# A new order of the steps on each engine, with margins behind the transposing DMAs

## The chip, the cores and the metric

The kernel runs on one core of a Trainium2 chip. The metric is the device time of one execution in microseconds (us). A core has TensorE (PE; its weight loads are listed as PEld), VectorE (DVE), ScalarE (ACT), GpSimd (POOL) and SyncE (SP), each of which works through its own list of instructions in order, and 16 DMA engines. Nearly all DMAs of this kernel are issued by SP. About 0.2% of the time is what a measurement of this kernel can tell from no change.

## The reference

The input x is 8 x 4160 x 192, with 8 heads of 24 channels. For each of the 33280 positions and each head, seven taps (softmax of `weight_gen` over the taps) weigh the position and the six before it. The result goes through a gated layer with 1024 hidden channels.

```python
w = softmax(weight_gen)                        # over 7 taps
a = einsum('bshk,bskhg->bshg', w, x_unf)       # x_unf: the position and six before it
h = a @ w_in                                   # 192 -> 1024
e = exp(h - max(h)); sm = e / (sum(e) + 1e-9)
solu = h * sm
ln = (solu - mean(solu)) / sqrt(var(solu) + 1e-6) * g_ln
out = ln @ w_out                               # 1024 -> 192
```

## The kernel before

Each of the 128 partitions holds a run of 260 consecutive positions. Position t of all runs together is tile t: 128 rows, one of each partition. x and `weight_gen` come in chunks of 16 tiles (a first one of 4), so the work repeats every 16 tiles.

For each group of four tiles (pairs at the start) POOL multiplies x by the taps (step `attA`, line 180) and adds part of the seven products (`attB`, L195); for some groups DVE adds the rest (`fin`, L461). PE turns two tiles at a time (`xT`, L477; where more than one product is left it sums them as it turns them), ACT and DVE split the result into two f16 parts (`xhi` L487, `xld` L491), and two small DMAs make a copy with halves swapped (`sw`, L497).

Then each tile t runs through this chain:

- `mm1` (PE, L511 and L516): the first product, 12 matmuls into a PSUM tile h, of which there are three.
- `max` (DVE, L528), `exp` (ACT, L534), `solu` (DVE, L542), `sq` (ACT, L548).
- `hi` (ACT, L555) and `lo` (DVE, L559) write h as two f16 halves into a tile `hl`, of which there are three. So `hi` of tile t may start only when the transpose of tile t-3 has landed, and `mm1` of tile t+3 only when `sq` and `lo` of tile t are done.
- `tr` (SP, L567): a DMA that transposes `hl` (128 x 2048 f16) into `hlT`, of which there are six.
- `mm2` (PE, L607): the second product, 24 matmuls from `hlT` into the one PSUM tile po; `out` (ACT, L618) scales it and frees po for the next `mm2`; `od` (SP, L622) stores four tiles.

Small steps `f0` to `f5` (ACT and DVE on `stats`) work out scales for four tiles, `v0` to `v5` and `t0` to `t6` prepare a chunk (L109 to L169; `t6` on POOL, L124, waits for `t5` on DVE, L122), and SP loads the next chunk in one piece for the taps (`lw`, L93) and four for x (`lx0` to `lx3`, L87).

The order of the steps on each engine is not written out by hand. `plan` lists all steps with engine, an assumed duration and what each comes after. `issue_order` then plays them through: each engine takes, of the steps whose predecessors are done by its own account, the one with the lowest key. The key is t plus a number from the table `URGENCY` (by the name of the step, or by name and tile for tiles 0 to 11). Of a DMA its account is a queue: for `tr` 625 ns in the queue, 650 ns, 1792 ns of transfer behind earlier transfers, and 950 ns, some 4.0 us when nothing else is under way. `MARGIN` adds to the time at which a step counts as ready, by the first two letters of the step before it and of its own, for tiles above 11:

```python
late = MARGIN.get((step[0][:2], to[0][:2]), 0) if to[1] > 11 else 0
...
key = [round(t + URGENCY.get(f"{name}_{t}", URGENCY.get(name, 0)), 6) for name, t, *_ in steps]
...
add("hi", t, ACT, 907, ("solu", t), ("tr", t - 3))
add("lo", t, DVE, 1140, ("hi", t))
add("tr", t, SP, 1792, ("lo", t), ("mm2", t - 6))
```

The order that comes out is issued; the instructions of a step, their tiles and their semaphores' sense do not depend on it.

Of the kernel before, what the change touches and what calls it, by code (L numbers as in the profile page):

```python
# [26 lines left out]
def tile_kernel(ctx: ExitStack, tc: tile.TileContext, x, weight_gen, w_in, w_out, g_ln, out):  # L27
# [646 lines left out]


URGENCY = dict(
    a00=105.6, a01=-44.5, a02=-89.4, a03=47.5, a04=67.9, a10=-22.3, a11=-196.9, a12=96.5, a13=145.9,
    a14=177.2, attA=54.9, attA_0=-160.1, attA_2=-41.9, attA_4=31, attA_6=-19.2, attA_8=-123.4,
    attB=-205.9, attB_0=-169, attB_2=78.4, attB_4=68.1, attB_6=172.9, attB_8=18.9, b0=179.7,
    b1=203.8, b2=103.9, b3=75.4, b4=-60.5, c00=230, c01=36.5, c02=-94.8, c10=16.599, c11=-151.7,  # L680
    c12=-32.1, c20=111.7, c21=-219.8, c22=-108.5, c30=95.7, c31=-78.4, c32=-191, dup=57.3,
    dup_0=0.9, dup_2=-49.2, dup_4=18.3, dup_6=109.3, dup_8=-102.8, exp=-77.6, exp_0=-74.8, exp_1=45,
    exp_10=41.6, exp_11=-71, exp_2=128.8, exp_3=106.7, exp_4=86.8, exp_5=-4.3, exp_6=-75.7,
    exp_7=-4.1, exp_8=-11.5, exp_9=-3.7, f0=160.2, f0_1=3.2, f0_11=-40.2, f0_3=20.6, f0_5=24.8103,
    f0_7=114.5, f1=-36.7, f1_1=-165.1, f1_11=-170.3, f1_3=-0.6, f1_5=-249.6, f1_7=167.7, f2=49.2,
    f2_1=-243.1, f2_11=-14, f2_3=-69.7, f2_5=-55.4, f2_7=179.9, f3=-243.7, f3_1=141.5, f3_11=-172.4,
    f3_3=-104.6, f3_5=-83.7, f3_7=-40.4, f4=-134.3, f4_1=132.7, f4_11=233.9, f4_3=241.4,
    f4_5=-100.1, f4_7=-19.9, f5=-125.6, f5_1=-121.6, f5_11=2.6, f5_3=5, f5_5=-56.4, f5_7=-110,
    fin=191.2, hi=31, hi_0=-142.6, hi_1=103.6, hi_10=-67.5, hi_11=90.6, hi_2=221.7, hi_3=74.4,
    hi_4=28.6816, hi_5=-54.3, hi_6=-41.8, hi_7=89.3, hi_8=154, hi_9=-98.6, lo=127.7, lo_0=21.7,  # L690
    lo_1=-24.2, lo_10=112.1, lo_11=-179.4, lo_2=56.8, lo_3=-11.4, lo_4=89.3, lo_5=-8.3, lo_6=-21.9,
    lo_7=-247.5, lo_8=-163.7, lo_9=-44.9, lw=-190.9, lx0=18.1, lx1=-49.4, lx2=186.6, lx3=-8.2,
    max=153.7, max_0=79.6, max_1=121.7, max_10=198.3, max_11=-116.8, max_2=99.9, max_3=-205.4,
    max_4=174.9, max_5=186.6, max_6=59.1, max_7=-243.1, max_8=-234.1, max_9=-26, mm1=-16.5,
    mm1_0=98.6, mm1_1=32.3, mm1_10=-45.3, mm1_11=-44.6, mm1_2=-182.6, mm1_3=41, mm1_4=177.5,
    mm1_5=188, mm1_6=-114.6, mm1_7=55.6, mm1_8=-65.6, mm1_9=77.9, mm2=-9, mm2_0=190.3, mm2_1=43.9,
    mm2_10=168.7, mm2_11=-13, mm2_2=-182.9, mm2_3=-48.7, mm2_4=-38.6, mm2_5=106, mm2_6=-59.1,
    mm2_7=134.4, mm2_8=184.4, mm2_9=28.1, n0=-101, n1=180.7, n2=115.5, n3=-82.1, n4=-13.1, n5=-87.1,
    n6=41.8, n7=-57.7, nq=-111.6, od=-168.9, od_11=48.8, od_3=202.8, od_7=-0.7, out=-68.9,
    out_0=179.4, out_1=69.3, out_10=214.4, out_11=-86.2, out_2=-19.4632, out_3=122.7, out_4=79.1,  # L700
    out_5=42.2, out_6=30.8, out_7=-123.8, out_8=56.1, out_9=-24.6, p30=-124.8, p31=-234.5, p4=69.7,
    p5=-12, p6=71.4, p70=134.1, p71=57.4, p80=-77.1, p81=-139.6, p9=14.5, q00=187.9, q01=203.8,
    q02=-72.2, q10=3.2, q11=70.5, q12=-1.9, q20=-26.1, q21=-76.9, q22=-33.3, q30=0.1, q31=13,
    q32=-12.7, solu=-183.4, solu_0=31.5, solu_1=-72.3, solu_10=71.4, solu_11=-178.3, solu_2=-78.7,
    solu_3=132.8, solu_4=-28.5, solu_5=58.6, solu_6=156.9, solu_7=65.1, solu_8=-95.3, solu_9=137.7,
    sq=98.5, sq_0=84.5, sq_1=61.5, sq_10=107.4, sq_11=-148.9, sq_2=72.8, sq_3=214.1, sq_4=15.9,
    sq_5=20.8, sq_6=76.5, sq_7=-91.5, sq_8=243.3, sq_9=135.1, sw=184.3, sw_0=150, sw_10=2.4,
    sw_2=180.1, sw_4=195.8, sw_6=116.8, sw_8=-155.7, t0=112.6, t0_0=1.1, t0_4=-124.5, t1=176.6,
    t1_0=-41, t1_4=49.9, t2=55.9, t2_0=-140.2, t2_4=145.3, t3=-133.3, t3_0=-99.3, t3_4=75.3,
    t4=87.9, t4_0=147.5, t4_4=41.3, t5=-14.2, t5_0=75.8, t5_4=58.5, t6=10.8, t6_0=-64.7, t6_4=-82.4,  # L710
    tr=-16.4, tr_0=-96.7, tr_1=-162.1, tr_10=190.2, tr_11=-176.7, tr_2=-146.3, tr_3=-51.4,
    tr_4=-237.3, tr_5=-44.8, tr_6=5, tr_7=65.2, tr_8=226.7, tr_9=-111.3, v00=-103.7, v00_0=107.8,
    v00_4=-243.9, v01=34.5, v01_0=140.6, v01_4=-205.3, v02=110.9, v02_4=155.8, v03=118,
    v03_4=-117.1, v1=-95.7, v1_0=-136.3, v1_4=-116.9, v2=54.7, v2_0=-48.6, v2_4=138.2, v3=154.5,
    v3_0=-43.2, v3_4=46.8, v4=167.3, v4_0=0.4, v4_4=101, v5=175.4, v5_0=68.5, v5_4=-56.5, w0=-17.7,
    w1=136.2, x0=13.6, x1=-60.7, xT=-189.8, xT_0=-82.9, xT_10=12.1, xT_2=-42.7, xT_4=57.1,
    xT_6=-124.6, xT_8=-5.9, xhi=-9.1, xhi_0=-36.3, xhi_10=30.9, xhi_2=54.2, xhi_4=1.6, xhi_6=-85.3,
    xhi_8=-197.1, xld=247.4, xld_0=-3.8, xld_10=59.3, xld_2=138.7, xld_4=-134.5, xld_6=-25.9,
    xld_8=-1.3,
)  # L720


# [207 lines left out]
def held(t):  # L930
# [8 lines left out]
}  # L939


# [102 lines left out]
```

## Time and profile before

| | us |
|---|---|
| median of 3 runs | 1261.78 (1260.18 to 1262.72) |
| the profiled execution | 1261.43 |
| its span, first to last instruction | 1259.7 |

Busy share of the span: PE 95%, DVE 91%, POOL 91%, ACT 89%. A share is an average: at the start PE waits for the weights and the first groups, and in the last stretch POOL has nothing left to do. In between the work repeats with each chunk of 16 tiles, so a chunk is the natural unit to compare: how long it takes, how much of that PE is busy, and which wait makes one chunk longer than another. The instruction of DVE that adds up the last products of a group (L461) appears once at the same place of each chunk on the chain that ended last, and its start marks the chunks in the rows below.

### The profile page before, as it was taken

Reading aid. Unit: us, or ns where it says so; the run is one execution under the profiler, and the core shown is the slowest. Engines: PE = TensorE matmul, PEld = TensorE weight load, DVE = VectorE, ACT = ScalarE, POOL = GpSimd, SP = SyncE. Lnnn points to the kernel's source line nnn. Section 1 sums busy time; section 2 is a strip of 40 time slices with the busy share of each in tenths; the row PEclk is TensorE's granted clock in tenths of the full one; section 3 lists DMA queues with packets and bytes.
Section 4 is the critical chain, followed back from the end, with each engine's and each line's share of the span. In section 5 each row is a group of like instructions: output and inputs, shape, how many; then the busy total and the mean of one; then the engine's idle time right before and its main releaser. Section 6 shows DMA issues by size and latency. Waiting matters only on the chain.

```text
span 1259.7 us, 27355 instructions
## 1 busy us (share of the span) xinstructions
PE 1196.3 (95%) x10296; PEld 820.8 (65%) x10296; DVE 1151.4 (91%) x1777; ACT 1124.0 (89%) x2286; POOL 1140.3 (91%) x235
## 2 busy tenths in 40 slices
PE   2899999999999999999999999999999999999997
PEld 2466666666666666666666666666666666766667
DVE  7788989989999998999999999989999998999983
ACT  6689999988999999899999989989998999988885
POOL 5999999999999999999999999998999999999300
PEclk9899999999999999999999999999999999999999
DMA  7579797987979788797989879797998969868765
GB/s 241 120 172 220 143 215 147 194 158 171 205 142 222 154 194 164 171 211 140 224 158 191 175 165 205 144 213 151 188 177 176 207 138 210 151 140 145 149 148 122
DMA packets 585491, 219.18 MB, mean 174 GB/s; under 512 B 548623, under 2 KB 566031, under 8 KB 585102
## 3 DMA queue, kind: packets, MB, share of 16 engines
q1 hardware_dynamic: 585056, 216.32, 82.9%
q8 instruction: 81, 1.33, 0.4%
q10 hardware_dynamic: 302, 1.11, 0.3%
q14 instruction: 52, 0.43, 0.1%
HBM read 45.60 MB, written 25.56 MB: 56 GB/s over the span
## 4 chain that ended last, share of the span: by engine, by line
ACT 31%; PE 25%; DVE 21%; issue 13%; DMA 8%; POOL 1%; ACTq 0%; SPq 0%; DVEq 0%; POOLq 0%
PE po L607 9%; ACT hl L555 9%; ACT e L534 9%; PE h L516 7%; ACT e L548 7%; DMA hlT<-hl 7%; DVE h L542 6%; DVE hl L559 6%; PE h L511 4%; DVE h L528 4%; DVE a L461 4%; PE pa L477 3%; ACT ot L618 2%; ACT stats L594 1%; ACT junk L145 1%
## 5 line engine op out<-in xcount | busy, mean ns | idle before, releaser
L180 POOL TENSOR_TENSOR pr<-xt,wt 128x5376 f32<-128x5376 f32 (+1 forms) x67 | 631.2, 9420 | 0.2
L607 PE MATMUL po<-w_hl,hlT 128*128 128x192 f16 x6168 | 554.0, 247 | 21.4 <-ACT ot L618 20.1
L607 PEld LDWEIGHTS <-hlT 128*128 128x128 f16 x6240 | 525.2, 98 | 71.5 <-issue 33.2
L195 POOL TENSOR_TENSOR pr<-pr 128x2304 f32<-128x2304 f32 (+1 forms) x122 | 449.6, 3686 | 7.3
L559 DVE SCALAR_TENSOR_TENSOR hl<-h,hl 128x1024 f16<-128x1024 f32 x260 | 316.8, 1220 | 43.5 <-ACT hl L555 24.2
L555 ACT ACTIVATE hl<-h 128x1024 f16<-128x1024 f32 x260 | 267.4, 1029 | 90.0 <-DVE h L542 44.1
L528 DVE TENSOR_SCALAR_CACHE_REDUCE h<-h,row 128x1024 f32<-128x1024 f32 x260 | 334.0, 1285 | 11.3 <-PE h L516 10.5
L542 DVE SCALAR_TENSOR_TENSOR h<-h,row,e 128x1024 f32<-128x1024 f32 x260 | 333.8, 1285 | 10.7 <-ACT e L534 7.7
L534 ACT ACTIVATE e<-h,stats 128x1024 f32<-128x1024 f32 x260 | 292.1, 1123 | 5.6 <-DVE h L528 5.4
L548 ACT ACTIVATE e<-h,stats 128x1024 f32<-128x1024 f32 x260 | 291.9, 1123 | 1.3 <-DVE h L542 1.1
L516 PEld LDWEIGHTS <-xh 128*128 128x128 f16 x1560 | 131.5, 98 | 234.2 <-issue 111.8
L516 PE MATMUL h<-w_odd,xh 128*128 128x512 f16 x780 | 190.9, 381 | 0.0
L516 PE MATMUL h<-wa_hi,xh 128*128 128x512 f16 x520 | 178.2, 384 | 0.0
L618 ACT ACTIVATE ot<-po,stats 128x192 f32<-128x192 f32 x257 | 110.5, 430 | 10.2 <-PE po L607 10.1
L511 PE MATMUL h<-w_odd,turned 64*128 64x512 f16 x390 | 106.4, 380 | 4.8 <-DVE hl L559 2.7
L511 PE MATMUL h<-w_odd,xh 64*128 64x512 f16 x390 | 106.7, 380 | 0.0
L511 PE MATMUL h<-wb_hi,xh 64*128 64x512 f16 x260 | 99.5, 383 | 6.4 <-DVE hl L559 3.1
L477 PE MATMUL pa<-ident,pr 128*128 128x128 f32 x738 | 94.7, 276 | 6.6 <-POOL pr L180 4.3
L511 PE MATMUL h<-wb_hi,turned 64*128 64x512 f16 x260 | 99.6, 383 | 0.8 <-DMA turned<-xh 0.8
L516 PE MATMUL h<-wa_lo,xh 128*128 128x512 f16 x260 | 99.1, 381 | 0.0
L477 PEld LDWEIGHTS pa<-ident,pr 128*128 128x128 f32 x738 | 84.5, 143 | 14.4 <-POOL pr L180 5.2
L511 PEld LDWEIGHTS <-turned 64*128 64x128 f16 x780 | 54.2, 94 | 43.6 <-issue 23.8
(90 smaller groups left out, 1001.7 us busy)
## 6 DMA issues: line engine op xcount, KB each, us to landing
out_dram<-ot SPq DMA_DIRECT2D x64, 384.0 KB, 3.2
xt<-in_x_dram SPq DMA_DIRECT2D x30, 576.0 KB, 4.9
xt<-in_x_dram SPq DMA_DIRECT2D x30, 480.0 KB, 4.6
turned<-xh SPq DMA_DIRECT2D x260, 32.0 KB, 2.5
wt<-in_weight_gen_dram SPq DMA_DIRECT2D x16, 448.0 KB, 4.5
hlT<-hl SPq DMA_TRANSPOSE x260, 4.6
xt<-in_x_dram SPq DMA_DIRECT2D x1, 1536.0 KB, 10.9
pr<-in_moe_w_out_dram SPq DMA_DIRECT2D x1, 1024.0 KB, 8.2
```

What stands on the lines that cost most here:

```text
L180: nc.gpsimd.tensor_tensor(out=window(pr, 0, [(ROW, K), (HG, n * H), (1, HG)]), in0=window(xt, t * D, [(D, K), (HG, n * H), (1, HG)]), in1= ...
L195: nc.gpsimd.tensor_tensor(out=b, in0=b, in1=a, op=ALU.add)
L477: nc.tensor.matmul(pa[:, k], source[:, first : first + P], ident, is_transpose=True, start=at == 0, stop=at == 3 * len(sources) - 1,)
L511: nc.tensor.matmul(h[:, fs], last[(f + odd) % 2][rows, low], rhs[rows], start=n == 0, stop=False)
L516: nc.tensor.matmul(h[:, fs], xh[:, 2 * odd, low], rhs[:, fs], start=False, stop=n == 2)
L528: nc.vector.tensor_scalar(h, h, row(t, BACK), 3.0e38, op0=ALU.mult, op1=ALU.min, accum_out=stat(t, NMAX))
L534: nc.scalar.activation(e, h_of[t], AF.Exp, bias=stat(t, NMAX), scale=-1.0, accum_out=stat(t, Z))
L542: nc.vector.scalar_tensor_tensor(out=h, in0=h, scalar=row(t, SCALE), in1=e, op0=ALU.mult, op1=ALU.mult, accum_out=stat(t, M))
L548: nc.scalar.activation(e_of.pop(t), h_of[t], AF.Square, bias=stat(t, M), scale=-float(FF), accum_out=stat(t, Q),)
L555: nc.scalar.activation(hl[:, 0, :], h_of[t], AF.Copy, scale=2.0**14)
L559: nc.vector.scalar_tensor_tensor(out=hl[:, 1, :], in0=h_of[t], scalar=2.0**14, in1=hl[:, 0, :], op0=ALU.mult, op1=ALU.subtract,)
L607: nc.tensor.matmul(po[:, :D], hlT[:, half * NJ + j, :], w2_hl[:, j, w, :], start=n == 0, stop=n == len(terms) - 1,)
```

## The change

All numbers of `URGENCY` that belong to a step that exists are drawn anew, save some that stay as they were, and `MARGIN` gets two more entries: behind `tr`, 2500 ns ahead of `hi` and 2000 ns ahead of `mm2` (the letters "mm"). No step is added, removed or altered; only the order in which the engines' instructions, SP's DMAs among them, are issued. The names that the diff leaves at the same number are partly names that no step has. Core of the diff, first the lines of the table that hold the keys of the chain, of SP's steps and of PE's:

```diff
@@ URGENCY = dict(
...
-    fin=191.2, hi=31, hi_0=-142.6, hi_1=103.6, hi_10=-67.5, hi_11=90.6, hi_2=221.7, hi_3=74.4,
-    hi_4=28.6816, hi_5=-54.3, hi_6=-41.8, hi_7=89.3, hi_8=154, hi_9=-98.6, lo=127.7, lo_0=21.7,
...
-    lo_7=-247.5, lo_8=-163.7, lo_9=-44.9, lw=-190.9, lx0=18.1, lx1=-49.4, lx2=186.6, lx3=-8.2,
-    max=153.7, max_0=79.6, max_1=121.7, max_10=198.3, max_11=-116.8, max_2=99.9, max_3=-205.4,
...
+    f5_5=-56.4, f5_7=130, fin=85.7, hi=-31.1, hi_0=2.9, hi_1=90, hi_10=111.9, hi_11=202.5,
...
+    lo=-87, lo_0=-144.9, lo_1=33.8, lo_10=-216.8, lo_11=-104.9, lo_2=-4.8, lo_3=81.7, lo_4=89.7,
+    lo_5=26.6, lo_6=75.2, lo_7=-43.1, lo_8=5, lo_9=-108.5, lw=94.3, lx0=12.4, lx1=-31.5, lx2=-203.1,
+    lx3=99.1, max=54.6, max_0=-76, max_1=-140.8, max_10=170.3, max_11=205.2, max_2=-63.7,
...
@@ MARGIN = {
     ("lx", "v0"): 6000, ("lw", "t0"): 6000, ("lx", "at"): 6000, ("t0", "t1"): 6000,
     ("t1", "t2"): 3000, ("t2", "t3"): 3000, ("t3", "t4"): 3000, ("v2", "t4"): 3000,
     ("t5", "t6"): 6000, ("sw", "mm"): 6000, ("xl", "sw"): 1500, ("mm", "tr"): 1000,
+    ("tr", "hi"): 2500, ("tr", "mm"): 2000,
 }
```

Other keys that the text below speaks of, before and after: `exp` -77.6 and 97.9, `out` -68.9 and -0.5, `sq` 98.5 and 118.2, `solu` -183.4 and -63, `xld` 247.4 and 114, `tr` -16.4 and -106.8, `od` -168.9 and 73.8, `sw` 184.3 and 6.4, `mm1` -16.5 and -18.1, `mm2` -9 and -10.1.

## Rows read from the trace of the kernel before

**Rows 1.** The page, part 1: busy time of each engine and its share.
```profile
PE 1196.3 (95%) x10296; PEld 820.8 (65%) x10296; DVE 1151.4 (91%) x1777; ACT 1124.0 (89%) x2286; POOL 1140.3 (91%) x235
```

**Rows 2.** Windows by chunk: stretch, its length, busy us per engine, granted clock, DMA.
```profile
220.60:297.04 76.44, 73.19 (x628) 50.17 (x626) 70.02 (x108) 67.94 (x139) 75.97 (x16) 0.98 0.87 173
...
444.02:518.44 74.42, 71.90 (x627) 49.08 (x625) 69.84 (x108) 67.80 (x139) 71.21 (x15) 1.00 0.85 178
...
590.92:662.84 71.92, 71.68 (x627) 48.98 (x625) 69.67 (x109) 67.96 (x139) 71.26 (x15) 1.00 0.89 183
...
810.89:886.61 75.72, 73.45 (x627) 50.16 (x625) 70.03 (x108) 68.02 (x139) 71.21 (x15) 0.98 0.88 174
...
sum 812.70, PE 793.76 PEld 542.00 DVE 768.50 ACT 746.61 POOL 791.15; mean PE 72.16 PEld 49.27 DVE 69.86 ACT 67.87 POOL 71.92
```

**Rows 3.** Waits, whole span: who waited for whom, us in total, times, longest us.
```profile
ACT hl L555 <- DVE h L542: 44.1, 41, 1.7
...
DVE hl L559 <- ACT hl L555: 24.2, 28, 3.4
ACT hl L555 <- DMA hlT<-hl: 21.9, 12, 3.5
...
PE po L607 <- ACT ot L618: 20.1, 19, 3.0
...
PE h L511 <- DVE hl L559: 5.8, 18, 1.5
```

**Rows 4.** Waits in the quiet chunk, 590.92 to 662.84 us.
```profile
ACT hl L555 <- DVE h L542: 2.4, 2, 1.6
...
DVE hl L559 <- ACT hl L555: 0.3, 1, 0.3
```

**Rows 5.** Timeline of ACT, DVE, PE at 477 to 481 us: start, us, what, [idle before].
```profile
477.70 1.02 ACT L555 ACTIVATE hl<-h 128x1024 f16<-128x1024 f32 x1 [2.71 <-DMA hlT<-hl]
...
479.99 0.42 ACT L618 ACTIVATE ot<-po,stats 128x192 f32<-128x192 f32 x1
...
478.76 1.22 DVE L559 SCALAR_TENSOR_TENSOR hl<-h,hl 128x1024 f16<-128x1024 f32 x1 [2.47 <-ACT hl L555]
...
480.46 2.14 PE L607 MATMUL po<-w_hl,hlT 128*128 128x192 f16 x24 [2.07 <-ACT ot L618]
```

**Rows 6.** Timeline of SP's DMA issues, 446 to 479 us; x2 are merged ones.
```profile
450.94 1.10 SPq L93 DMA_DIRECT2D wt<-in_weight_gen_dram  x1
452.15 3.28 SPq L567 DMA_TRANSPOSE hlT<-hl  x1
...
469.63 7.53 SPq L567 DMA_TRANSPOSE hlT<-hl  x2
```

**Rows 7.** Timeline of DVE, 459 to 478 us: writers of the late transposed tiles.
```profile
466.35 2.44 DVE L559 SCALAR_TENSOR_TENSOR hl<-h,hl 128x1024 f16<-128x1024 f32 x2
```

**Rows 8.** Transposes issued at 469.6 us and from 480 to 516 us, to landing.
```profile
DMA to landing us min/median/max: 8.0/8.0/8.0
...
DMA to landing us min/median/max: 4.3/4.5/5.3
```

**Rows 9.** The page, part 6: DMA issues, KB each, median us to landing.
```profile
xt<-in_x_dram SPq DMA_DIRECT2D x30, 480.0 KB, 4.6
...
hlT<-hl SPq DMA_TRANSPOSE x260, 4.6
```

**Rows 10.** All transposes: who waited for them, in us and times.
```profile
  ACT hl L555: 21.9, 12
  PEld L511: 1.6, 10
```

**Rows 11.** Windows of the start, the tail, and six us behind one late transpose.
```profile
0.00:78.00 78.00, 47.04 (x323) 32.29 (x324) 60.64 (x98) 54.87 (x122) 64.27 (x27) 0.96 0.67 183
...
1177.50:1259.70 82.20, 74.22 (x693) 54.74 (x691) 57.22 (x90) 59.81 (x115) 0.00 (x1) 1.00 0.67 140
256.00:262.00 6.00, 3.99 (x30) 3.22 (x29) 5.62 (x8) 6.00 (x13) 6.00 (x1) 0.72 0.93 179
```

More of the change, by code (lines that the diff above doesn't have):

```diff
@@ L676 @@
 URGENCY = dict(
[L677 to L688, printed above, removed]
@@ L689 @@
-    fin=191.2, hi=31, hi_0=-142.6, hi_1=103.6, hi_10=-67.5, hi_11=90.6, hi_2=221.7, hi_3=74.4,
-    hi_4=28.6816, hi_5=-54.3, hi_6=-41.8, hi_7=89.3, hi_8=154, hi_9=-98.6, lo=127.7, lo_0=21.7,
-    lo_1=-24.2, lo_10=112.1, lo_11=-179.4, lo_2=56.8, lo_3=-11.4, lo_4=89.3, lo_5=-8.3, lo_6=-21.9,
-    lo_7=-247.5, lo_8=-163.7, lo_9=-44.9, lw=-190.9, lx0=18.1, lx1=-49.4, lx2=186.6, lx3=-8.2,
-    max=153.7, max_0=79.6, max_1=121.7, max_10=198.3, max_11=-116.8, max_2=99.9, max_3=-205.4,
-    max_4=174.9, max_5=186.6, max_6=59.1, max_7=-243.1, max_8=-234.1, max_9=-26, mm1=-16.5,
@@ L695 @@
[L695 to L718, printed above, removed]
@@ L719 @@
-    xld_8=-1.3,
+    a00=135.6, a01=-100.6, a02=-89.7, a03=156.4, a04=135.7, a10=-35.1, a11=-109.1, a12=-28.5,
+    a13=95.8, a14=-55.7, attA=-121, attA_0=-17.6, attA_2=98, attA_4=210, attA_6=198.2,
+    attA_8=-119.9, attB=142.6, attB_0=143.6, attB_2=-21.5, attB_4=-149.1, attB_6=-174.9, attB_8=4.4,
+    b0=243.1, b1=143.7, b2=-162.8, b3=159.7, b4=112.5, c00=148.9, c01=54, c02=85.9, c10=184.8,
+    c11=-182.8, c12=-186.8, c20=21.6, c21=186, c22=50, c30=95.7, c31=-78.4, c32=-191, dup=57.3,
+    dup_0=0.9, dup_2=-49.2, dup_4=18.3, dup_6=109.3, dup_8=-102.8, exp=97.9, exp_0=-72.9,
@@ new lines @@
+    exp_1=110.7, exp_10=-95.8, exp_11=92.8, exp_2=-18.9, exp_3=-5.8, exp_4=9.8, exp_5=87.6,
+    exp_6=-55.5, exp_7=-82.3, exp_8=99.3, exp_9=178.2, f0=130.8, f0_1=3.2, f0_11=-213.8, f0_3=117.1,
+    f0_5=24.8103, f0_7=-143.5, f1=24.2, f1_1=-165.1, f1_11=73.8, f1_3=115.4, f1_5=-249.6,
+    f1_7=-205.6, f2=100.7, f2_1=-243.1, f2_11=2.6, f2_3=-16, f2_5=-55.4, f2_7=-34, f3=-28.7,
+    f3_1=141.5, f3_11=79.1, f3_3=105.8, f3_5=-83.7, f3_7=-123.8, f4=-235.3, f4_1=132.7, f4_11=130.1,
+    f4_3=-41.4, f4_5=-100.1, f4_7=215.4, f5=-115.5, f5_1=-121.6, f5_11=-129.6, f5_3=55.6,
@@ new lines @@
+    f5_5=-56.4, f5_7=130, fin=85.7, hi=-31.1, hi_0=2.9, hi_1=90, hi_10=111.9, hi_11=202.5,
+    hi_2=-109, hi_3=-28, hi_4=18.6, hi_5=-166.9, hi_6=214, hi_7=143.4, hi_8=-33.4, hi_9=-112.3,
+    lo=-87, lo_0=-144.9, lo_1=33.8, lo_10=-216.8, lo_11=-104.9, lo_2=-4.8, lo_3=81.7, lo_4=89.7,
+    lo_5=26.6, lo_6=75.2, lo_7=-43.1, lo_8=5, lo_9=-108.5, lw=94.3, lx0=12.4, lx1=-31.5, lx2=-203.1,
+    lx3=99.1, max=54.6, max_0=-76, max_1=-140.8, max_10=170.3, max_11=205.2, max_2=-63.7,
+    max_3=-35.5, max_4=22.9, max_5=89.3, max_6=-40.4, max_7=-213.5, max_8=-220.8, max_9=17.3,
@@ new lines @@
+    mm1=-18.1, mm1_0=23.8, mm1_1=-171, mm1_10=-41, mm1_11=-80.2, mm1_2=-27.5, mm1_3=-10.7,
+    mm1_4=-32.8, mm1_5=14.3, mm1_6=27.6, mm1_7=-75.4, mm1_8=-2.2, mm1_9=190.2, mm2=-10.1,
+    mm2_0=-121.8, mm2_1=-11.3, mm2_10=-67.6, mm2_11=-12.1, mm2_2=171.8, mm2_3=122.5, mm2_4=135.5,
+    mm2_5=117.3, mm2_6=-7.4, mm2_7=28.5, mm2_8=-68.1, mm2_9=32.7, n0=-35.6, n1=-21.6, n2=82.6,
+    n3=-82.1, n4=123.5, n5=-87.1, n6=-188.9, n7=91.3, nq=-111.6, od=73.8, od_11=-160, od_3=-70.3,
+    od_7=-4.3, out=-0.5, out_0=183.2, out_1=-44.7, out_10=-132.5, out_11=-175, out_2=166.1,
@@ new lines @@
+    out_3=198.1, out_4=-63.1, out_5=-212.7, out_6=50, out_7=-91.1, out_8=51.5, out_9=230.6,
+    p30=167.1, p31=147.3, p4=-212.4, p5=-12.2, p6=-34.3, p70=137.7, p71=-13.7, p80=-155.6, p81=23.5,
+    p9=-81.9, q00=51.6, q01=93, q02=195.6, q10=-76.6, q11=82.6, q12=76.2, q20=207.5, q21=-15.7,
+    q22=34.6, q30=-99.6, q31=-129.1, q32=-33.5, solu=-63, solu_0=-51.6, solu_1=-168.1,
+    solu_10=-215.2, solu_11=-110.6, solu_2=122.4, solu_3=-186.8, solu_4=52.3, solu_5=-7.8,
+    solu_6=-89.2, solu_7=152.7, solu_8=16, solu_9=216.4, sq=118.2, sq_0=106, sq_1=-5.4, sq_10=116.6,
@@ new lines @@
+    sq_11=110.7, sq_2=-127.8, sq_3=83.7, sq_4=38.3, sq_5=-137.3, sq_6=52.1, sq_7=23.7, sq_8=4.3,
+    sq_9=-118.7, sw=6.4, sw_0=2.2, sw_10=-33, sw_2=-1.1, sw_4=-26.2, sw_6=-149.3, sw_8=71.1,
+    t0=132.6, t0_0=11.9, t0_4=-51.5, t1=101, t1_0=56.2, t1_4=-6.3, t2=148.6, t2_0=60.2, t2_4=246.7,
+    t3=74, t3_0=-11, t3_4=49.9, t4=-67.1, t4_0=-120.7, t4_4=43.6, t5=57.8, t5_0=-30.5, t5_4=28.4,
+    t6=6.4, t6_0=8.8, t6_4=101.4, tr=-106.8, tr_0=-114.7, tr_1=-76.9, tr_10=172.6, tr_11=-67,
+    tr_2=-23.9, tr_3=-81.4, tr_4=34.2, tr_5=-49.9, tr_6=95.9, tr_7=-142.4, tr_8=-9.2, tr_9=-25.4,
@@ new lines @@
+    v00=25.4, v00_0=129.2, v00_4=-107.8, v01=62.9, v01_0=-48.3, v01_4=163.7, v02=121, v02_4=-77.8,
+    v03=74.2, v03_4=43.9, v1=53.2, v1_0=52.3, v1_4=-17, v2=94.2, v2_0=-187, v2_4=-10.6, v3=154.9,
+    v3_0=-140.1, v3_4=114.4, v4=79.6, v4_0=-150.9, v4_4=237.1, v5=-39.2, v5_0=49.1, v5_4=136.3,
+    w0=22.6, w1=10.6, x0=-19.4, x1=111.9, xT=-24.965, xT_0=29.4, xT_10=-83.3, xT_2=154, xT_4=-51,
+    xT_6=188.4, xT_8=148.4, xhi=-205.9, xhi_0=-1.6, xhi_10=28, xhi_2=-13.4, xhi_4=-101.8, xhi_6=7.8,
+    xhi_8=-207.3, xld=114, xld_0=-59.4, xld_10=55.1, xld_2=20.2, xld_4=-115.4, xld_6=84.3,
@@ L720 @@
+    xld_8=26.7,
 )
```

## The prediction

> **What bounds the kernel now.** Read the busy shares first: PE 95%, DVE, POOL and ACT 89 to 91% [rows 1]. Four engines this close together say little by their averages, so go to the windows cut at the chunks [rows 2]. Of the eleven chunks from 220.60 to 1033.30 us the mean takes 812.70 / 11 = 73.88 us and the shortest 71.92 us. In the shortest PE is busy for 71.68 us, all but 0.24: there PE is the bound, with POOL right behind (71.26), then DVE (69.67) and ACT (67.96). PE's busy time hardly differs in the other chunks (71.90 in one of 74.42 us), except in the two with a granted clock of 0.98, where it is 73.19 and 73.45. So a chunk costs what PE needs, some 71.7 us, plus waits of PE, and the waits are what a new order can change.
>
> Which waits those are is in the list of waits [rows 3]. Rows with large sums are not all on the path: of the 44.1 us of ACT at `hi` for DVE the shortest chunk has its share of 2.4 [rows 4]. What differs is ACT at `hi` waiting for the transposing DMA, 21.9 us in 12 times, longest 3.5 [rows 3]. The timeline of one case shows what hangs on it [rows 5]: `hi` starts at 477.70 after 2.71 us of idle ACT. DVE has `lo` next in its list and waits 2.47. `out`, which stands behind `hi` on ACT, comes at 479.99, and since po is a single tile PE's `mm2` starts 2.07 us late. The 20.1 us of PE for `out` [rows 3] I take to be largely this: one late transpose stops three engines, once in nearly every chunk.
>
> Then why the transpose is late. From 450.94 us SP issues the loads of a chunk, small copies, a store and transposes in one row without a pause [rows 6] (the first two and the last of 13 rows stand there), and an issue of a transpose occupies SP for 3 to 4 us there. The `hl` of the late one was written by the first of two `lo` that follow each other from 466.35 us (2.44 together, so it ended at about 467.6) [rows 7]. Its issue came at 469.63 [rows 6], 2.0 us behind, and it landed 8.0 us later, where those of the quiet stretch behind it take 4.3 to 5.3, median 4.5 [rows 8]. So it is 2.0 us late at SP and 8.0 - 4.5 = 3.5 in flight: 5.5 us in all.
>
> **The change, part by part.** No instruction is added or removed, so every engine's work stays as it is [rows 1]; all of the effect is in waits.
>
> (a) The margin of 2.5 us from `tr` to `hi`. The planner now counts `hi` as ready 2.5 us after its own landing time. In the case above the old order would have run `hi` 2.71 us earlier, so it allowed for 5.5 - 2.7 = 2.8 us over a quiet landing. If all of that allowance was slack in the planner's account, it already met the margin and nothing changes: 0. If all of it was queueing that the planner had counted itself (it charges 1540 ns for each part of x), the margin comes on top, and of twelve waits with a mean of 21.9 / 12 = 1.8 us nearly all go. What a chunk gains then is bounded by the shortest chunk: 73.88 - 71.92 = 1.96 us, over eleven chunks 21.6 us. That includes the clock: behind the longest late transpose the clock granted in 256 to 262 us was 0.72 [rows 11], which is part of what lengthens PE's work in two chunks by (73.19 - 71.9) + (73.45 - 71.9) = 2.8 us [rows 2].
>
> (b) The margin of 2.0 us from `tr` to `mm2`. Those who waited for a transposed tile are ACT at `hi` and, with 0.2 us each, a weight load of the first product; `mm2` is not among them [rows 10]. The margin guards a wait that doesn't occur: 0. It costs a later place of `mm2`, for which there are six `hlT` tiles; bound 0 to one `mm2`, 2 us once, at the end.
>
> (c) The keys. A lower key goes first among steps that are ready. `lo` goes from 127.7 (behind `solu`, -183.4) to -87, in front of `solu`, `max` and `xld`; `hi` from behind `exp` and `out` to in front of both. Tiles already under way are finished first, so `hl` is written sooner and `tr` issued sooner, which works in the same direction as (a). On SP `tr` (-106.8) now stands in front of `lw`, `od`, `sw` and three parts of x, where before `lw` and `od` stood in front. The planner frees SP after 60 ns, whereas the trace shows 3 to 4 us for a transpose [rows 6], so its queue hardly ever has two steps to choose between and I count this as nothing. `mm1` and `mm2` stay 8 tiles apart in their keys (7.5 before), so PE's alternation should remain.
>
> (d) Start and tail. For tiles 0 to 11 no margin applies, but the order is drawn anew. PE is busy 47.04 of the first 78 us, and 74.22 of the 82.20 behind POOL's last instruction [rows 11]. Most of the former is the wait for weights, which no order shortens. For both together I take 0, between -4 (half of the tail's 8 us of idle PE) and +4 (the same in the other direction, no row excludes it).
>
> The sum: of the 21.6 us of (a) and (c) I take 60%, 13 us. The value lies nearer to the full end, since nearly all the waits are shorter than the margin; not at it, because 5.5 us of lateness is more than 2.5, and the burst of loads must still fall somewhere. 1261.4 (the profiled execution; 0.35 below the median of the runs, 1261.78) - 13 = 1248 us.
>
> A rule that speaks against it. A transpose lands in 4.6 us by median, and so does a part of x of 480 KB [rows 9]; in the burst the one at 469.63 took 8.0 [rows 8]. The Trainium skill, page Advanced Engine Details and Errata, section X-Bar Transpose (TRN2), says that on TRN2 transposing DMAs are as fast as regular ones. By that page the transpose isn't what is slow, and the trace's medians agree: the crowd of DMAs is late as a whole. Padding behind transposes alone would then move the collision to another place instead of ending it, which is the second rival.
>
> **The rivals.**
>
> 1. Full recovery. Every chunk becomes the shortest one: 1261.4 - 21.6 = 1240 us, and 1238 with part of the tail. For: PE, POOL and DVE already fitted into 71.92 us once. Against: it leaves POOL 71.92 - 71.26 = 0.7 us of slack in a chunk, so the order has to be nearly perfect and nothing else late.
>
> 2. The wait moves. The burst of loads falls on other transposes or on `sw` or `t0`, and some step that ACT or DVE has in front waits 1 to 3 us once a chunk as before: 1261 us, within 0.2%. For: the SP issues block each other [rows 6], which the planner's 60 ns doesn't see. It is also what happens if the old order already met the margin.
>
> 3. Slower: `lo` in front blocks DVE. With `lo` ahead of `solu` and `max`, DVE stands still whenever `hi` comes later than planned, and `mm1` three tiles on waits for `lo` (already 5.8 us in 18 times [rows 3]). In the quiet chunk `lo` waits for `hi` once, 0.3 us [rows 4], and DVE has 71.92 - 69.67 = 2.25 us to spare. The kernel gets slower where DVE's waits exceed 73.88 - 69.86 = 4.0 us a chunk: sixteen `lo` that wait 0.3 us each make 4.8, so 0.8 us a chunk too much, some 10 us over thirteen chunks: 1271 us. For: DVE's own mean over the chunks leaves just these 4 us. Against: `lo` counts as ready only once `hi` is done, so in the plan it blocks nobody; it takes real lateness at many tiles.
>
> **How the numbers follow.** Forecast (1242 to 1257) 0.50; full recovery (below 1242) 0.13; the wait moves (1259.3 to 1264.3) 0.15; slower (1264 to 1276) 0.22. With 0.2% as what can be told from no change, faster holds 0.63, same 0.15, slower 0.22. The range reaches to 1238 at the lower end (full recovery, and half of what the tail could give) and to 1268 at the upper (the middle of the slower case), leaving out about 0.05 and 0.12.
>
> **What would show it.** Right: the wait of ACT at `hi` for the transpose falls from 21.9 to below 8 us, that of PE for `out` from 20.1 to some 8, the eleven chunks sum to about 800 us with PE's busy time still at 71.7 to 71.9 each and a granted clock of 1.00 in all of them. Rival 2: the chunk stays near 73.9 and another row of DMA takes the place. Rival 3: DVE at `lo` for ACT above 24.2 us, and more of PE for `lo`. The forecast is wrong in its mechanism if the wait for the transpose goes and the chunk doesn't get shorter; and wrong in (d) if chunks behave as forecast but the first 126 or the last 82 us differ by over 4 us.

## The result and the profile after

The changed kernel takes 1245.11 us (median of 4 runs, 1243.28 to 1248.37) against 1262.25 us before (1260.18 to 1263.85 in the runs beside it): a ratio of 0.9868, 95% interval 0.9842 to 0.9894. That is 17 us faster; the forecast was 1248. The profiled execution took 1243.28 us with a span of 1241.5, so its span is 18.2 us shorter than before.

First the page after, part 1 (busy us, share of the span, instructions), against [rows 1]:

```profile
PE 1188.7 (96%) x10296; PEld 818.6 (66%) x10296; DVE 1151.7 (93%) x1777; ACT 1127.1 (91%) x2286; POOL 1140.1 (92%) x235
```

The instructions are the same and so, but for a few us, is the busy time; PE's is 7.6 us less. Now the windows after, cut at the same DVE instruction (L461) as [rows 2]: stretch, length, busy us of PE, PEld, DVE, ACT and POOL, granted clock, DMA share, GB/s; the first three of eleven chunks and the sum.

```profile
220.93:295.47 74.54, 73.66 (x637) 49.86 (x635) 72.22 (x115) 70.53 (x145) 74.07 (x15) 1.00 0.86 181
295.47:366.62 71.15, 69.35 (x612) 48.10 (x610) 67.50 (x106) 65.91 (x136) 70.68 (x15) 1.00 0.88 182
366.62:441.76 75.14, 74.13 (x640) 50.01 (x639) 71.95 (x113) 70.18 (x144) 74.67 (x16) 1.00 0.88 180
...
sum 797.46, PE 790.25 PEld 540.57 DVE 770.01 ACT 750.90 POOL 790.56; mean PE 71.84 PEld 49.14 DVE 70.00 ACT 68.26 POOL 71.87
```

The new order repeats every two chunks, so the lengths alternate, and only pairs compare. The last ten chunks take 797.46 - 74.54 = 722.92 us, 72.29 each; before they took 812.70 - 76.44 = 736.26 [rows 2], 73.63 each. That is 13.3 us. Of the rest of the 18.2, the chunk ahead of these ten gives 76.44 - 74.54 = 1.9 (a single one, to be read with care), everything ahead of 220 us loses 0.3, and the stretch behind the eleven chunks gives 3.3: before, 1259.7 - 1033.30 = 226.4; after, 1241.5 - 1018.39 = 223.1. The granted clock is 1.00 in all the chunks; before it was 0.98 in two.

The waits after, over the whole span, against [rows 3] (us in total, times, longest):

```profile
DVE hl L559 <- ACT hl L555: 24.7, 47, 2.3
...
ACT hl L555 <- DVE h L542: 20.9, 33, 1.4
...
PE h L511 <- DVE hl L559: 11.7, 13, 5.4
...
PE po L607 <- ACT ot L618: 6.9, 13, 1.7
...
ACT hl L555 <- DMA hlT<-hl: 6.1, 8, 1.7
```

ACT's wait at `hi` for the transpose fell from 21.9 to 6.1 us and PE's for `out` from 20.1 to 6.9. The transposes themselves did not come sooner. Of all 260, from issue to landing (min, median, max); before, the median was 4.6 [rows 9] and the one of the example took 8.0 [rows 8]:

```profile
DMA to landing us min/median/max: 4.2/4.9/8.4
```

What changed is how long the order leaves them. Here is the same tile as in [rows 5 to 7], after: its `lo` on DVE, its transpose on SP (two issues merged, the first is the one), and the `hi` three tiles on, on ACT.

```profile
461.66 1.21 DVE L559 SCALAR_TENSOR_TENSOR hl<-h,hl 128x1024 f16<-128x1024 f32 x1
```
```profile
466.57 6.67 SPq L567 DMA_TRANSPOSE hlT<-hl  x2
```
```profile
472.56 1.14 ACT L548 ACTIVATE e<-h,stats 128x1024 f32<-128x1024 f32 x1
...
473.64 1.06 ACT L555 ACTIVATE hl<-h 128x1024 f16<-128x1024 f32 x1
```

`lo` ends at 462.87. The transpose is issued 3.7 us behind that, later than before (2.0), and lands 6.4 us after its issue, 10.1 us behind `lo`; before it landed 8.0 us after its issue, 10.1 us behind `lo` as well. Yet `hi` starts without an idle gap in front of it at 473.64, 10.8 us behind `lo`. Before, ACT came to this `hi` at 477.70 - 2.71 = 474.99, 7.4 us behind the `lo` that ended at about 467.6. The new order gives this transpose 3.4 us more. The same place of the other chunks (tiles 41, 57 and so on to 217, this one is 89) shows the same: from the end of `lo` to the time at which ACT comes to the `hi` three tiles on, 10.6 to 11.7 us pass after and 7.4 to 8.1 passed before, while these transposes land 10.1 to 12.5 us behind `lo` after and 7.3 to 11.0 before. So the new order bears a lateness that it does not lessen.

### The profile page after: what moved, and what is told of

Its sections match the earlier page's. It is cut to its first block, busy times and chain, and to the rows that moved or that the text cites. A ratio compares the mean times of both kernels' runs of the same rounds, so it can differ in the third digit from the quotient of the medians.

```text
span 1241.5 us, 27360 instructions
## 1 busy us (share of the span) xinstructions
PE 1188.7 (96%) x10296; PEld 818.6 (66%) x10296; DVE 1151.7 (93%) x1777; ACT 1127.1 (91%) x2286; POOL 1140.1 (92%) x235
## 5 line engine op out<-in xcount | busy, mean ns | idle before, releaser
L607 PEld LDWEIGHTS <-hlT 128*128 128x128 f16 x6240 | 522.8, 98 | 52.6 <-issue 10.6
L559 DVE SCALAR_TENSOR_TENSOR hl<-h,hl 128x1024 f16<-128x1024 f32 x260 | 316.4, 1221 | 41.6 <-ACT hl L555 24.7
L511 PEld LDWEIGHTS <-xh 64*128 64x128 f16 x780 | 53.7, 94 | 47.1 <-issue 22.6
```

The source lines that it names most:

```text
L511: nc.tensor.matmul(h[:, fs], last[(f + odd) % 2][rows, low], rhs[rows], start=n == 0, stop=False)
L559: nc.vector.scalar_tensor_tensor(out=hl[:, 1, :], in0=h_of[t], scalar=2.0**14, in1=hl[:, 0, :], op0=ALU.mult, op1=ALU.subtract,)
L607: nc.tensor.matmul(po[:, :D], hlT[:, half * NJ + j, :], w2_hl[:, j, w, :], start=n == 0, stop=n == len(terms) - 1,)
```

## The experiments

Each run's ratio is to the kernel before on the same chip, with its 95% interval. Where the text speaks of 192 tiles, it means the time from the start of the 28th `max` on DVE to that of the 220th, twelve chunks' worth of the repeating part: 884.7 us in the kernel before, 869.0 in the changed one.

**Margins or keys.** The changed kernel without the two margins:

```diff
-    ("tr", "hi"): 2500, ("tr", "mm"): 2000,
```

> The changed kernel with the two margins behind the transposes taken out again; the new keys stay, so the planner makes another order. Theory M (the margins make the difference, by giving hi more time behind the transpose): most of the gain goes, 1253 to 1262 us, and ACT's wait at hi for the transpose comes back to 15 us or more (before 21.9, changed 6.1). Theory K (the newly drawn keys make it, the margins are incidental): 1243 to 1249 us as the changed kernel, and that wait stays at 10 us or below.

Measured: 1246.39 us, 0.9886 (0.9867 to 0.9905), the wait at `hi` for the transpose 8.4 us. Not to be told from the changed kernel. Reading the two orders against each other, instruction by instruction, shows why: they differ in one place, a single `hi` near the end that goes in front of a `sq`. With the new keys the planner makes this order with or without the margins.

The other half, the old keys with the margins:

```diff
+    ("tr", "hi"): 2500, ("tr", "mm"): 2000,
```

> The kernel before with its own keys and only the two margins added. Theory M: 1244 to 1254 us, the wait at hi for the transpose below 10 us. Theory K: no gain or a loss, 1258 to 1275 us, since the keys were not chosen for these margins; if the wait at hi for the transpose falls all the same, other waits must take its place.

Measured: 1284.46 us, 1.0188 (1.0171 to 1.0206): 24 us slower. Its waits:

```profile
DVE h L542 <- ACT e L534: 27.4, 42, 2.1
ACT e L534 <- DVE h L528: 24.0, 23, 3.5
PE po L607 <- ACT ot L618: 23.8, 30, 2.0
...
PE h L511 <- DVE hl L559: 20.0, 31, 1.5
...
ACT hl L555 <- DMA hlT<-hl: 3.7, 4, 2.2
```

The margin does what it is meant to: 3.7 us instead of 21.9 at `hi`. But the order that the planner then makes is another one on all engines, and PE waits more for `out` and for `lo` than before [rows 3], and DVE for `exp`. The 192 tiles take 902.5 us instead of 884.7: the wait at `hi` goes and the chunks get longer all the same. Of the two margins only the one ahead of `hi` does this; with the one ahead of `mm2` alone the old keys give the old order, the same on every engine. In both runs it is the theory of the keys that holds, here with a loss beyond the 1275 us that it allowed.

**Is it the wait at all?** The kernel before with four `hl` tiles, so that `hi` waits for the transpose of four tiles earlier, its order untouched:

```diff
-        hl = hl_of[t] = big.tile([P, 2, FF], F16, name="hl", bufs=3)
+        hl = hl_of[t] = big.tile([P, 2, FF], F16, name="hl", bufs=4)
...
-            junk = small.tile([P, HALO * D], F32, name="junk", bufs=1)
+            junk = small.tile([P, HALO * D], F16, name="junk", bufs=1)
```

> The kernel before, order of steps unchanged, with four hl tiles instead of three, so that hi waits for the transpose of four tiles earlier and no longer for a late one (to make room, the tile junk, which nothing reads, is f16 instead of f32). Theory W (the gain of the change is the wait of hi for late transposes, and what hangs on it): the wait goes to about 0, PE's wait for out from 20.1 to below 6 us, and the time to 1240 to 1247 us, as the changed kernel. Theory R (the late transpose only shows a stop that another limit would cause anyway: POOL, DVE or the next wait): 1253 us or more.

Measured: 1238.50 us, 0.9825 (0.9806 to 0.9844), just below the range of theory W and faster than the changed kernel's median by 6.6. PE's wait for `out` is 6.3 us (below 6 was expected), that of `hi` for the transpose is no longer in the list. The windows, two of eleven chunks and the sum:

```profile
292.92:364.85 71.93, 71.68 (x626) 48.97 (x625) 69.71 (x110) 68.01 (x139) 71.46 (x15) 1.00 0.91 185
...
868.39:940.34 71.95, 71.69 (x627) 48.99 (x625) 69.72 (x110) 68.02 (x139) 71.48 (x15) 1.00 0.92 184
...
sum 791.29, PE 788.55 PEld 538.94 DVE 766.79 ACT 748.00 POOL 786.12; mean PE 71.69 PEld 48.99 DVE 69.71 ACT 68.00 POOL 71.47
```

Every chunk takes what the shortest one took before [rows 2]: the sum fell by 812.70 - 791.29 = 21.4 us, where the shortest chunk had promised 21.6. All that made chunks differ was this one wait and what hangs on it. The squares that write `junk` take the same time in f16 (865 ns against 866), so that edit is not the cause.

The changed kernel with the same edit:

> The changed kernel with four hl tiles (and junk in f16), its order unchanged. Theory W: what is left of the wait at hi for the transpose, 6.1 us, of which PE feels some 2.5 us in the chunks, goes: 1240 to 1244 us, little better than the changed kernel. Theory R: no difference, 1244 to 1247 us. If it beats the kernel before with four hl by more than 3 us, the new order is better by something else than by these waits.

Measured: 1237.87 us, 0.9821 (0.9804 to 0.9837). It wins 7 us more, rather than the 1 to 5 expected, and comes out level with the kernel before with four `hl`. Of the two orders with four `hl` the new one takes 864.5 us for the 192 tiles and the old one 863.3, so in the repeating part the new order is worth nothing by itself. What it is worth there is that it bears late transposes with three tiles: it gains 884.7 - 869.0 = 15.7 of the 884.7 - 863.3 = 21.4 us that the fourth tile gains, some three quarters.

**Why the transposes are late.** The kernel before with every DMA issued as before, but with few bytes in the chunk's loads:

```diff
+            if c > 3:
+                r1 = r0 + 1
             nc.sync.dma_start(xv[:, r0:r1, :], x_run[:, t0 - HALO + r0 : t0 - HALO + r1, :])
...
+        n = 1 if c > 3 else n
         nc.sync.dma_start(wv[:, :n, :], w_run[:, t0 : t0 + n, :])
```

> The kernel before with the same DMAs in the same order, but from the fifth chunk on the loads of x and of the taps move one row of positions instead of five or six (x) or sixteen (taps), so most of the tiles hold old data: the loads' bytes are left out, their issues stay. Theory L (the transposes are late because the chunk's loads share the DMA engines with them): landings of the transposes over 5.5 us nearly vanish (before 59 of 260), the wait at hi for them falls from 21.9 to below 4 us, and the time to 1238 to 1246 us. Theory Q (they are late because SP issues one DMA behind the other, whatever the bytes): the wait stays at 10 us or more and the time above 1252 us.

Measured: 1238.67 us, 0.9818 (0.9791 to 0.9844). Who waited for the transposes, and their landings (the line numbers are five higher here):

```profile
  PEld L516: 1.6, 10
  ACT hl L560: 1.4, 1
...
DMA to landing us min/median/max: 4.2/4.4/6.6
```

One wait of 1.4 us is left, at a `hi` near the end that waited 1.2 us before too. One sign of theory L did not come: landings over 5.5 us did not nearly vanish, they fell from 59 to 32 of 260. What went is the lateness that `hi` felt. It comes with the bytes of x and taps; the same number of issues on SP does no harm without them. That the bytes compete for the DMA engines, rather than for something else on their way, is likely (their busy share is 0.85 to 0.89 in the chunks of [rows 2]) but was not tested by itself.

The changed kernel with the same loads:

> The changed kernel with the same loads left out in the same way. If the changed kernel's gain is tolerance of late transposes and nothing else, it has little left to win here: 1238 to 1243 us, within 3 us of the kernel before with light loads. If its order were better also without lateness, it would be 4 us or more below that one.

Measured: 1236.36 us, 0.9802 (0.9769 to 0.9835), somewhat below the range given and 2.3 us below the kernel before with light loads, within the 3 us set. The 192 tiles take 863.6 us here and 863.4 there, so the repeating part says the same as with four `hl`, and the 2.3 us lie in the start and the end.

**Can it be had by moving one step?** The kernel before, with the `hi` that waits put behind the next `out` on ACT in 14 chunks; the edit works on the finished order:

```diff
+    for t in range(28, 252, 16):
+        i = act.index(("hi", t))
+        j = next(n for n in range(i, len(act)) if act[n][0] == "out")
+        act.insert(j, act.pop(i))
```

> The kernel before with one step moved in each of 14 chunks: the hi that waits for the late transpose goes behind the next out in ACT's order, that is behind some 1.8 us of ACT's work; the orders of PE, DVE, SP and POOL are as before. Theory W: PE's wait for out falls from 20.1 to below 8 us, ACT's at hi from 21.9 to below 10; DVE still waits at lo, but has 2 us to spare in a chunk: 1243 to 1251 us. Theory R (DVE's stop is what counts, or hi later costs as much): 1256 us or more.

Measured: 1271.43 us, 1.0077 (1.0049 to 1.0105): slower, a miss for theory W; theory R holds. ACT no longer waits there (1.4 us in all), but look at the timeline of one chunk on DVE, ACT and PE:

```profile
405.56 1.22 DVE L559 SCALAR_TENSOR_TENSOR hl<-h,hl 128x1024 f16<-128x1024 f32 x1 [2.50 <-ACT hl L555]
```
```profile
406.82 1.11 ACT L548 ACTIVATE e<-h,stats 128x1024 f32<-128x1024 f32 x1 [1.29 <-DVE hl L559]
```
```profile
408.07 0.37 PE L511 MATMUL h<-w_odd,turned 64*128 64x512 f16 x1 [0.93 <-ACT e L548]
411.00 0.55 PE L477 MATMUL pa<-ident,a 128*128 128x128 f32 x3 [0.70 <-DVE a L461]
```

`lo` is next on DVE and stops it for 2.50 us, now in every chunk and not only where a transpose is late; then `sq` waits for `lo`, and PE for `sq` and for the sum behind it on DVE. The seven chunks from 222 to 742 us take 74.3 to 74.6 us (before, 73.88 on average); one of them:

```profile
444.92:519.18 74.26, 72.09 (x626) 49.17 (x625) 69.73 (x110) 68.13 (x139) 71.23 (x15) 1.00 0.86 178
```

So the same with `lo` moved too, behind the next `solu` on DVE:

```diff
+        i = dve.index(("lo", t))
+        j = next(n for n in range(i, len(dve)) if dve[n][0] == "solu")
+        dve.insert(j, dve.pop(i))
```

> The kernel before with hi behind the next out on ACT, as in the run that moved hi alone, and now lo of the same tile behind the next solu on DVE too, in the same 14 chunks; PE, SP and POOL keep their orders. Theory D (moving hi alone failed because lo stayed at the head of DVE's order and stopped DVE 2.5 us a chunk; ACT and DVE have to be moved together): DVE's wait at lo for hi falls from 40.6 to below 15 us, the chunks come to 71.9 to 72.8 us, and the time to 1239 to 1252 us. Theory F (a later hl costs as much as the late transpose, wherever it stands, through the three PSUM tiles h that wait for lo or through the transposes behind): 1258 us or more.

Measured: 1266.14 us, 1.0033 (1.0022 to 1.0045), still some 4 us slower than before. DVE's wait at `lo` for ACT is gone as expected (11.8 us in all), and still the chunk takes 74.2 us, theory F. What stays, on ACT and PE:

```profile
405.15 1.11 ACT L548 ACTIVATE e<-h,stats 128x1024 f32<-128x1024 f32 x1 [1.29 <-DVE hl L559]
```
```profile
406.41 0.37 PE L511 MATMUL h<-w_odd,turned 64*128 64x512 f16 x1 [0.95 <-ACT e L548]
409.55 2.14 PE L607 MATMUL po<-w_hl,hlT 128*128 128x192 f16 x24 [0.59 <-ACT ot L618]
```

`sq` still comes behind `lo`, and `mm1` three tiles on needs the PSUM tile that both read. The hand moves replace a loss that differs from chunk to chunk (73.88 - 71.92 = 1.96 us on average) by one of some 2.3 us in every chunk. Neither of the two made `hi` later without a new wait behind it; the changed order, which does, has its neighbours on ACT, DVE and PE arranged anew. That no smaller move could do it is not shown.

**Is any order with these keys good?** The changed kernel with margins and keys, but the old keys for tiles 0 to 11, which sends the planner on another way throughout:

> The changed kernel with both margins and its own keys for the repeating part, but the old keys for tiles 0 to 11. The planner then makes another order throughout, one that nobody has chosen. Theory S (an order fits because it was chosen among many as a whole; margins and the keys of the repeating part don't make a good one by themselves): slower than the changed kernel by 10 us or more, 1255 to 1300 us. Theory P (the priorities lo and hi first, with the margins, are what is good): 1243 to 1252 us, with the chunks as in the changed kernel and only the start different.

Measured: 1312.13 us, 1.0404 (1.0373 to 1.0434). That is slower than either theory gave. Two stretches of it, the start and the 192 tiles:

```profile
0.00:150.00 150.00, 89.09 (x666) 59.90 (x667) 99.08 (x161) 96.56 (x209) 112.75 (x35) 0.89 0.62 152
```
```profile
203.00:1106.30 903.30, 866.29 (x7504) 594.34 (x7503) 839.55 (x1286) 824.77 (x1665) 874.61 (x173) 1.00 0.87 176
```

The span is 68 us longer than the changed kernel's. Some half of that, 31 us, is lost ahead of the 192 tiles (PE busy 89 of the first 150 us, granted clock 0.89), and 34 us in them: 903.3 us against 869.0, and 884.7 in the old order. The priorities of the repeating part and the margins do not make an order good. With the run of margins alone these are two orders that came of mixing old and new, both slower than the old one. That the old and the changed order are better because each was picked among many is not shown by any run.

**All runs side by side.** Where the time goes, by the profiled executions, in us:

| run | ahead of the 192 tiles | the 192 tiles | behind them |
|---|---|---|---|
| before | 169.7 | 884.7 | 205.2 |
| changed | 171.6 | 869.0 | 200.9 |
| changed, without the margins | 171.6 | 873.1 | 201.0 |
| before, with the margins | 169.4 | 902.5 | 209.4 |
| before, four `hl` | 170.2 | 863.3 | 203.8 |
| changed, four `hl` | 171.5 | 864.5 | 200.4 |
| before, light loads | 169.3 | 863.4 | 204.2 |
| changed, light loads | 170.4 | 863.6 | 200.3 |
| before, `hi` moved | 169.5 | 891.6 | 208.2 |
| before, `hi` and `lo` moved | 169.8 | 888.7 | 205.9 |
| changed, old keys for tiles 0 to 11 | 203.0 | 903.3 | 203.2 |

## Why the prediction was right, point by point

**The bound.** "A chunk costs what PE needs, some 71.7 us, plus waits of PE" held to a few tenths of a us: with four `hl` tiles all chunks took 71.93 to 71.95, with PE busy 71.7. The ceiling that came from the shortest chunk, 21.6 us, was measured as 21.4.

**(a), the size and the cause.** The forecast took 60% of the ceiling, 13 us, from the chunks. Ten chunks gave 13.3 us and the one ahead of them 1.9, 15.2 in all, so the size was about right. The step that put it to the margin as the planner applies it was not: taking the margins out changes one place in the finished order and no time that can be measured, and putting them into the old keys costs 24 us. Whether the margins had a part in how the new keys were found, no run here can tell. Of the two ends given for (a), "it already met the margin and nothing changes" is what is true of the new keys. With the old keys the other end came true for the waits, of which nearly all went (21.9 to 3.7 us), and the chunks still got longer: what (a) left out is that the margin makes the planner draw up the whole order anew. So the forecast had the wait that is saved and its bound right; that 60% of the bound, argued from the margin, met what the new keys gave is luck.

**(b)** was right: zero. The margin ahead of `mm2` changes no instruction's place with the old keys.

**(c)** "in the same direction as (a)" undersized the keys: they are the whole of the change. Which of them do it was not tested. The priorities read from the table, `lo` and `hi` first, were no explanation either, since the mixed keys have them too and their repeating part is slower than the old one. Nor were all of them new: `lo` (127.7) stood in front of `max` and `xld` before as well, and on SP `lx1` (-49.4) in front of `tr`. What counts is where the finished order places `hi`, 10.8 us behind `lo` instead of 7.4 in the example, and that wasn't to be read from the keys. "`tr` sooner" was wrong in the example: its wait for SP rose from 2.0 to 3.7 us.

**(d)** Start and tail at 0, within 4 us each way: the tail gave 3.3, the start lost 0.3. Both stretches are wider than those that the prediction named. The new order's end is shorter without late transposes too: behind the 192 tiles the two orders with four `hl` take 203.8 and 200.4 us, so this is the order's own. With the 2.2 us that the chunks gave beyond 13 it brought the time below the forecast.

**The rivals.** Full recovery did not come with three tiles (1245 against 1240), but did with four. The moved wait happened in part: most of the 6.1 us left sits at the same `hi`. The blocked DVE did not happen in the changed kernel (24.7 us against 24.2, in 47 short waits rather than 28). PE's wait for `lo`, the rival's other sign, rose from 5.8 to 11.7 us, but 5.4 of that is a single wait at 57.8 us, ahead of the repeating part. The mechanism exists, though: the run with one step moved shows it as described, `lo` in front stopping DVE, and at 1271 us. The Trainium skill, page Advanced Engine Details and Errata, section X-Bar Transpose (TRN2), says that transposing DMAs are as fast as regular ones on TRN2. The trace agrees as far as loads of like size go: 4.6 us by median for a transpose and for a part of x of 480 KB [rows 9]. The second rival's conclusion, that margins would only move the collision, missed that an order can leave the collision where it is and wait for it at a better time.

## What to carry to other kernels

In a loop bound by one engine, compare repetitions of the loop with each other: the shortest one prices the removable waits, here 21.6 us against 21.4 measured when the wait was taken away. Where a late DMA stops several engines through a buffer, try one more buffer before a better order: here 4 KB a partition gave 22 us, more than the 17 of the new order, and made the two orders equal. And the margins and priorities of a planner like this one are not dials: the same margin gave nothing with one set of keys and cost 24 us with another, so predict from the finished order, which the planner gives without a run on the chip, or not from them at all.

## What the runs showed of the hardware

With the bytes of the loads left out and the DMAs issued as before, the transposes land sooner: the longest time to landing fell from 8.0 to 6.6 us, with the median at 4.4 against 4.6. SP's issues get shorter too. The three transposes issued among the example's loads occupied SP for 3.28, 3.16 and 4.01 us before, and for 2.03, 1.81 and 2.77 us with light loads. I had put 2.0 of the example's 5.5 us of lateness to SP's issues; that part went with the bytes as well. With light loads the example's `lo` (the first of two merged ones) ends at about 459.5, its transpose is issued at 459.58 and lands 4.5 us later:

```profile
458.30 2.45 DVE L564 SCALAR_TENSOR_TENSOR hl<-h,hl 128x1024 f16<-128x1024 f32 x2
```
```profile
444.08 2.03 SPq L572 DMA_TRANSPOSE hlT<-hl  x1
...
459.58 4.66 SPq L572 DMA_TRANSPOSE hlT<-hl  x2
```

So bytes and issues, the two theories of that experiment, are not apart: SP's issues of transposes take longer while the loads' bytes are under way.
